# An MoE kernel in a hand-ordered schedule: counts that go from the scan to the triangular product, weights asked for at step 2, other pauses between engines, small products in banks of their own

## The chip, the cores and the metric

One core of one Trainium2 chip runs the whole program once. The metric is device microseconds of one launch. A profile is one further launch with the hardware profiler on; its times are taken from that launch alone.

## What is computed

Three layers follow one another on 14336 tokens of 192 numbers each (4 sequences of 3584).

```python
# 1  causal convolution over 7 tokens, one softmaxed filter per head (8 heads of 24)
out = einsum('hk,bskhg->bshg', softmax(weight), x_unf)
# 2  first MoE, on the tokens with x @ w_skip > 0 only; the others pass as they are
e_idx = argmax(xc @ w_gate); gate_w = softmax prob of e_idx
y[mask e] = gate_w * (relu(xc @ w1[e]) @ w2[e]); out = xc + y
# 3  second MoE, on all tokens
logits = x @ w_gate + modality_bias[modality_id]
out[mask e] = gate_w * (relu(x @ w1[e]) @ w2[e])
```

Each MoE has 8 experts with w1 of 192 x 1024 and w2 of 1024 x 192, and picks one expert for a token. All inputs are float32.

## The kernel before

**Data.** Products run in float16 with a high and a low part of each operand. The experts' weights are therefore prepared on the chip: for each expert the sum of squares is found by products of the weights with themselves (`gram`, a PSUM region), a power of two is taken from it as a scale, and the weights are split into a high and a low part (`w1b`, `w2b` for layer one, three buffers of each; `o` for layer two), which are also stored to DRAM (`s1a`, `s2a`, `s1b`, `s2b`) for the jobs that load them later.

**Stages.** The first phase (`Phase1.run`) goes through 64 convolution steps v (8 groups of 16 token tiles, 8 heads each) and 12 more to empty its pipeline: step v transposes the tiles of v - 9 (`tr`), convolves head v % 8 of group v // 8 (`conv`), and makes the gate products of v - 11 (`gm`); `lows` is VectorE's part, `fin` the gate decision of one group. Then `Ffn.run` goes through jobs of 128 tokens of one expert: 56 jobs of layer one and 6 overflow jobs (n1 = 62), then the jobs of layer two, first the tokens that skipped layer one (B), then those that came out of it (A). The first 12 jobs (experts 0 to 3, three jobs each) use tokens of the first four groups only, so that they can start before the first phase is through; jobs 12 to 55 take experts 1 to 7 and then 0. Each job is two first products with their evictions (`mm1`), and the second product of the job before (`mm2`).

**Order.** VectorE, ScalarE, TensorE and GpSimd execute their instructions in the order in which the program emits them (`InOrder`); SyncE, which issues the DMAs, is ordered by the compiler's scheduler. Background work is written as Python generators: a `yield n` lets n ticks pass. The first phase gives two ticks per step; `bg`, which a job calls four times, runs one step of the first phase while there are any left (`"x" not in w`), with that step's two ticks, and then ticks the queues `tk` (gates, routing) and `tkw` (weights) itself: `tk` twice in the first 12 jobs until the full routing is known, else once, `tkw` once. So the pauses fix where, among the products, each small operation stands in its engine's queue; an operation that is not ready there holds up all that is behind it on that engine.

**Routing.** `route_a` takes the gate codes of one group, compares them with the 8 experts (`oh`), scans the result over experts and tiles (`cum`, one running sum through all of them), and needs for each expert how many tokens of it lie in lower partitions: a product of the per-partition counts with a strictly triangular matrix (`tri`), and with ones for the totals. The counts are differences of neighbouring ends of the running sum, made on GpSimd (`genda`, `cnta`). From the product come ranks, slots and the index lists `la` (after 4 groups) and `ls` (after 8). `ranks` is the same for the other routes, on VectorE.

**Weights.** `prep` is one lane of weight preparation. For each expert in its list: loads (`loadt`, `loadr`, `load2`, the next expert's while the present one is split), products for the sums of squares, `dg` and `ssq` on VectorE, a product with ones, `pow2`, then the split in eight steps with `pace` ticks between, then the two stores. Lane 0 starts in step 8 of the first phase, lane 1 when the first phase is over (`late_pools`). A split waits for a free buffer (`guard`) and for the other lane's split (`busy`). If job i needs an expert of layer one that is not split yet, `pre` ticks `tkw` until it is: all that was still to come is then emitted at once, ahead of the job's products. At the end of job 56 (`i == n1 - 6`) `tk.drain` and `tkw.drain` do the same with whatever is left, and the pools of the second lane are given back.

**Banks.** PSUM has 8 banks, here `bk[0]` to `bk[7]`. Two engines' accesses to one bank are ordered one after the other, whichever columns they touch.

## Time and profile before

| | |
|---|---|
| three runs | 1071.69, 1083.71, 1078.73 us; median 1078.73 |
| the profiled execution | 1078.92 us, span 1077.1 us, mean granted clock 0.941 |
| busy: TensorE, VectorE, GpSimd, ScalarE | 967.9, 688.7, 628.5, 501.1 us |
| weight loads on TensorE (beside its products) | 802.2 us |
| DMA | 165.35 MB, mean 154 GB/s |

The span goes from the first to the last instruction; the execution's own time is 1.8 us longer. Busy time is the sum of the instructions of an engine. The granted clock is TensorE's: 1.00 is 2.4 GHz, and a stretch at 1.2 GHz counts 0.5. In the rows below PE is TensorE, DVE VectorE, ACT ScalarE, POOL GpSimd, SP SyncE; an operation is written as out<-in with the names of the program's tiles (`bank` is any PSUM bank), partitions x elements and type; what stands in brackets is the engine's idle time before it and who ended that. Nearly all instructions bear line 70, that of the helper that emits them, so tiles tell them apart.

### The profile page before, as it was taken

Reading aid. Unit: us, or ns where it says so; the run is one execution under the profiler, and the core shown is the slowest. Engines: PE = TensorE matmul, PEld = TensorE weight load, DVE = VectorE, ACT = ScalarE, POOL = GpSimd, SP = SyncE. Lnnn points to the kernel's source line nnn. Section 1 sums busy time; section 2 is a strip of 40 time slices with the busy share of each in tenths; the row PEclk is TensorE's granted clock in tenths of the full one; section 3 lists DMA queues with packets and bytes.
Section 4 is the critical chain, followed back from the end, with each engine's and each line's share of the span. In section 5 each row is a group of like instructions: output and inputs, shape, how many; then the busy total and the mean of one; then the engine's idle time right before and its main releaser. Section 6 shows DMA issues by size and latency. Waiting matters only on the chain. (4 is left out here: it accounts for less than half of the span.)

```text
span 1077.1 us, 27331 instructions
## 1 busy us (share of the span) xinstructions
PE 967.9 (90%) x10104; PEld 802.2 (74%) x10104; DVE 688.7 (64%) x1797; ACT 501.1 (47%) x919; POOL 628.5 (58%) x1113
## 2 busy tenths in 40 slices
PE   6688877799999879999899999999999899999993
PEld 4556666688888767888777877778787788888882
DVE  4376966769998889888446666667844344444441
ACT  3485743443665535455345555553233333333331
POOL 4044778776856836676447877774443555545531
PEclk9887876999999889999999999999999999999997
DMA  5666457665669737767973443333257333323340
GB/s 203 210 205 246 153 169 217 172 199 160 208 181 267 229 121 244 221 204 219 292 229 98 95 110 101 96 101 91 53 151 242 78 73 75 76 72 72 79 117 14
DMA packets 109135, 165.35 MB, mean 154 GB/s; under 512 B 80976, under 2 KB 86074, under 8 KB 103233
## 3 DMA queue, kind: packets, MB, share of 16 engines
q1 hardware_dynamic: 94368, 134.02, 39.9%
q0 software_dynamic: 13920, 28.87, 11.9%
q8 instruction: 81, 1.33, 0.5%
q10 hardware_dynamic: 704, 0.63, 0.2%
q14 instruction: 62, 0.50, 0.2%
HBM read 181.56 MB, written 58.42 MB: 223 GB/s over the span
## 5 line engine op out<-in xcount | busy, mean ns | idle before, releaser
L70 PEld LDWEIGHTS <-w1b 128*128 128x128 f16 x4840 | 374.4, 100 | 54.1 <-issue 18.5
L70 PE MATMUL bank<-xp,w1b 128*128 128x256 f16 x2200 | 263.7, 273 | 8.2 <-DMA w1b<-s1b 2.5
L70 PEld LDWEIGHTS <-ws 128*128 128x128 f16 (+2 forms) x2208 | 192.1, 100 | 67.0 <-DMA ws<-in_moe_w_dram 10.9
L70 PE MATMUL bank<-w2b,ws 128*128 128x384 f16 x1760 | 237.4, 286 | 0.2 <-issue 0.2
L70 DVE SCALAR_TENSOR_TENSOR ws<-bank,ws 128x512 f16<-128x512 f32 x220 | 151.4, 690 | 124.3 <-ACT ws L70 105.6
L70 POOL DMA_INDIRECT out_dram<-u,si x114 | 115.4, 1013 | 185.2 <-DVE u L70 58.7
L70 ACT ACTIVATE ws<-bank 128x512 f16<-128x512 f32 x220 | 130.6, 597 | 113.5 <-PE bank L70 102.7
L70 PE MATMUL bank<-xt,w1b 128*128 128x128 f16 x2640 | 170.1, 225 | 10.7 <-DVE hlo L70 6.9
L70 PE MATMUL bank<-w2b,hh 128*128 128x384 f16 x528 | 141.2, 334 | 1.0 <-DMA w2b<-s2a 1.0
L70 PE MATMUL bank<-w2b,hlo 128*128 128x192 f16 x528 | 131.8, 250 | 0.0
L70 ACT ACTIVATE u<-bank,c 128x192 f32<-128x192 f32 x114 | 48.1, 422 | 153.2 <-PE bank L70 118.1
L70 DVE SCALAR_TENSOR_TENSOR hlo<-bank,hh 128x512 f16<-128x512 f32 x132 | 90.3, 686 | 42.2 <-ACT hh L70 41.3
L70 DVE SCALAR_TENSOR_TENSOR u<-bank,c,u 128x192 f32<-128x192 f32 x114 | 47.6, 417 | 100.5 <-ACT u L70 84.5
L70 ACT ACTIVATE hh<-bank 128x512 f16<-128x512 f32 x132 | 76.7, 593 | 42.1 <-PE bank L70 40.7
L70 PEld LDWEIGHTS <-hh 128*128 128x128 f16 x528 | 53.4, 101 | 31.5 <-issue 3.3
L70 POOL DMA_INDIRECT gt<-rows,idx x64 | 64.0, 999 | 11.2 <-issue 9.3
L70 PE MATMUL bank<-xg,band 128*112 128x384 f32 x128 | 64.0, 593 | 0.3 <-DVE s L70 0.3
L70 ACT COPY xtb<-bank 128x672 f16<-128x672 f16 x64 | 46.5, 728 | 36.9 <-PE bank L70 36.5
L70 POOL DMA_INDIRECT gt<-rows,idxB x56 | 56.5, 1008 | 11.9 <-issue 7.0
L70 POOL TENSOR_TENSOR x2s<-x2s,xs 128x192 f32<-128x192 f32 x46 | 31.6, 688 | 53.7 <-DVE x2s L70 42.2
L70 PE MATMUL bank<-ob,oa 128*128 128x56 f16 (+2 forms) x446 | 49.7, 263 | 6.0 <-DVE ob L70 6.0
L70 PEld LDWEIGHTS <-hlo 128*128 128x128 f16 x528 | 52.9, 100 | 1.6 <-issue 1.5
(252 smaller groups left out, 1431.8 us busy)
## 6 DMA issues: line engine op xcount, KB each, us to landing
w1b<-s1b SPq DMA_DIRECT2D x59, 1024.0 KB
w2b<-s2b SPq DMA_DIRECT2D x59, 768.5 KB
ws<-in_moe_w_dram SPq DMA_DIRECT2D x16, 768.0 KB
rows<-hl SPq DMA_DIRECT2D x8, 1386.0 KB
xg<-in_x_dram SPq DMA_DIRECT2D x7, 1536.0 KB
ws<-in_moe_w_dram SPq DMA_DIRECT2D x16, 512.0 KB
ws<-in_moe_w_dram SPq DMA_DIRECT2D x32, 256.0 KB
s1a<-w1b SPq DMA_DIRECT2D x8, 1024.0 KB
```

What stands on the lines that cost most here:

```text
L70: r = f(*args, **kw)
```

## The change

In `route_a` and `ranks` the last column of the running sum itself goes into the two products, and the differences are taken of the results, after the copy out of PSUM (`off`, `po`, with a zero column in front). The first lane starts in step 2 and pauses 26 ticks before its first product, where it started in step 8 and paused 14; the second lane pauses 14 where it paused 8. Between VectorE's sums of squares and the product with ones lie 5 ticks (3 before), then 3 (2), then 3 (1) to the split. While layer one's jobs run and the first phase is not over, the split takes 2 ticks a step (1). `tk` is ticked twice a call only once the first phase is over. Expert 6 of layer two goes from the second lane's end to the first lane's end. `res["A"]`, which lets the next group's routing start, is set ahead of a pause. The second lane's sums of squares and the small routing products go to bank 4, and the last gate sums from bank 5 to bank 4. An unused region is dropped.

```diff
--- before.py
+++ after.py
@@ -33,7 +33,7 @@
 SB = 7
 NSA = E * SB
 XA = 16
-LANES = [(0, e) for e in range(E)] + [(1, 7)], [(1, e) for e in range(7)]
+LANES = [(0, e) for e in range(E)] + [(1, 7), (1, 6)], [(1, e) for e in range(6)]
 RW = 396
 MB = 192
 CAP = 120
@@ -124,16 +124,15 @@
         self.py = [bk[2][:, :2 * D]]
         self.py2 = bk[6][:, :2 * D]
         self.acc = [bk[3], bk[5]]
-        self.pt, self.pt2 = [h[4][:, 0:384]], [h[7][:, 512:896], h[3][:, 0:384]]
+        self.pt2 = [h[7][:, 512:896], h[3][:, 0:384]]
         self.pg2 = [bk[5][:, i:i + 64] for i in (0, 64, 128)]
-        self.gram = [bk[7][:, 256:512], bk[7][:, 0:256]]
-        self.misc = bk[3][:, 496:512]
+        self.gram = [bk[7][:, 256:512], bk[4][:, 0:256]]
+        self.misc = bk[4][:, 496:512]
         self.ph3 = bk[5]
         self.misca = bk[3][:, 240:256]
         self.pc0 = [bk[i][:TP, :384] for i in (5, 0, 1)]
         self.ptr0, self.ptr1 = ([h[i][:, :6 * TP] for i in p] for p in ((6, 2), (6, 5)))
-        self.pgt0, self.pgt1 = ([bk[i][:, 0:136] for i in p] for p in ((7, 4), (7,)))
-        self.pgt1.append(bk[5][:, 352:488])
+        self.pgt0, self.pgt1 = ([bk[i][:, 0:136] for i in p] for p in ((7, 4), (7, 4)))
         self.gramx = bk[3][:, 384:512]
         self.scm = bk[3][:, 256:384]
         self.cp = ctx.enter_context(tc.tile_pool(name="cp", bufs=1))
@@ -279,7 +278,7 @@
         nc.vector.tensor_scalar(out.bitcast(I32), q.bitcast(I32), -0.5, float(0x5F3759DF), ALU.mult, ALU.add)
         nc.vector.tensor_scalar(out.bitcast(I32), out.bitcast(I32), EXPM, None, ALU.bitwise_and)
 
-    def prep(self, ws, pool, pq, dst, guard, done, es, lane, lag, pace, free, busy):
+    def prep(self, ws, pool, pq, dst, guard, done, es, lane, lag, pace, free, busy, first):
         nc = self.nc
         g = self.gram[lane].rearrange("p (i c) -> p i c", i=2)
         sq = g[:, 0, 0:2]
@@ -301,7 +300,7 @@
             return w2t
 
         nxt = (loadt(*es[0]), loadr(*es[0])), load2(*es[0])
-        yield lag()
+        yield first
         for n, (q, e) in enumerate(es):
             (wt, wr), w2t = nxt
             for i, vs in enumerate(((wt,) * 8 + (wr[0:64],) * 8, (w2t,) * 12)):
@@ -315,13 +314,13 @@
             nc.vector.tensor_tensor(dg, g, self.identf.unsqueeze(1).to_broadcast([128, 2, 128]), ALU.mult)
             ssq = pq.tile([128, 2], F32, name="ssq")
             nc.vector.tensor_reduce(ssq, dg, AX.X, ALU.add)
+            yield 5
+            nc.tensor.matmul(sq, self.ones, ssq, start=True, stop=True)
             yield 3
-            nc.tensor.matmul(sq, self.ones, ssq, start=True, stop=True)
-            yield 2
             sc = pq.tile([128, 2], F32, name="wsc")
             self.pow2(sq, sc)
             nc.vector.tensor_scalar(sc, sc, 2.0 ** 30, 2.0 ** FT, ALU.min, ALU.mult)
-            yield 1
+            yield 3
             while not guard(q, e) or busy[0]:
                 yield 1
             busy[0] = True
@@ -361,15 +360,15 @@
             nc.vector.scalar_tensor_tensor(o1[:, 3, F // 2:], wr[:, F // 2:], sc[:, 0:1], o1[:, 2, F // 2:], ALU.mult, ALU.subtract)
             done[q].add(e)
             busy[0] = False
-            yield 2 + q
+            yield 2
             nc.sync.dma_start(ws[q][2][e], o1)
-            yield 2 + q
+            yield 2
             nc.sync.dma_start(ws[q][3][e], o2.bitcast(I32))
-            yield 2 + q
+            yield 2
             if q:
                 free[0] = None
             if not last:
-                yield max(1, lag() - 3 * (2 + q))
+                yield max(1, lag() - 6)
 
     def route_a(self, g, code, pool, ob, res):
         nc = self.nc
@@ -398,20 +397,21 @@
         gend = pool.tile([128, 9], F32, name="genda")
         nc.gpsimd.memset(gend[:, 0:1], 0.0)
         nc.gpsimd.tensor_copy(gend[:, 1:9], cum[:, :, GT - 1])
-        cnt = pool.tile([128, 8], F32, name="cnta")
-        nc.gpsimd.tensor_tensor(cnt, gend[:, 1:9], gend[:, 0:8], ALU.subtract)
+        off = pool.tile([128, 2, 9], F32, name="offa")
+        nc.gpsimd.memset(off[:, :, 0:1], 0.0)
         pos = pool.tile([128, GT], F32, name="posa")
         nc.gpsimd.tensor_scalar(pos, cg, -float(SB * 128), float(8 * SB * 128), ALU.mult, ALU.add)
+        yield 4
+        pp = self.misca
+        nc.tensor.matmul(pp[:, 0:8], self.tri, cum[:, :, GT - 1], start=True, stop=True)
+        nc.tensor.matmul(pp[:, 8:16], self.ones, cum[:, :, GT - 1], start=True, stop=True)
         yield 3
-        pp = self.misca
-        nc.tensor.matmul(pp[:, 0:8], self.tri, cnt, start=True, stop=True)
-        nc.tensor.matmul(pp[:, 8:16], self.ones, cnt, start=True, stop=True)
-        yield 2
-        off = pool.tile([128, 16], F32, name="offa")
-        nc.vector.tensor_copy(off, pp)
+        nc.vector.tensor_copy(off[:, :, 1:9], pp.rearrange("p (k c) -> p k c", k=2))
+        cnt = pool.tile([128, 2, 8], F32, name="cnta")
         nc.gpsimd.tensor_tensor(gend[:, 0:8], base, gend[:, 0:8], ALU.subtract)
-        nc.gpsimd.tensor_tensor(gend[:, 0:8], gend[:, 0:8], off[:, 0:8], ALU.add)
-        nc.gpsimd.tensor_tensor(base, base, off[:, 8:16], ALU.add)
+        nc.gpsimd.tensor_tensor(cnt, off[:, :, 1:9], off[:, :, 0:8], ALU.subtract)
+        nc.gpsimd.tensor_tensor(gend[:, 0:8], gend[:, 0:8], cnt[:, 0], ALU.add)
+        nc.gpsimd.tensor_tensor(base, base, cnt[:, 1], ALU.add)
         if g == GA - 1:
             nc.gpsimd.tensor_scalar(base[:, 0:EA], base[:, 0:EA], float(SA * 128), None, ALU.max)
         nc.gpsimd.tensor_tensor(cum, cum, gend[:, 0:8].unsqueeze(2).to_broadcast([128, 8, GT]), ALU.add)
@@ -437,8 +437,8 @@
         nc.gpsimd.tensor_tensor(q, pos, tf, ALU.add)
         nc.gpsimd.tensor_tensor(ok[:, 0], ok[:, 0], cg, ALU.mult)
         nc.gpsimd.tensor_tensor(cg, cg, ok[:, 0], ALU.subtract)
+        res["A"] = g + 1
         yield 5
-        res["A"] = g + 1
         for h in (2 * g, 2 * g + 1):
             u = slice(8 * (h % 2), 8 * (h % 2) + 8)
             a = ob.tile([128, 128, 8], F16, name="oa", bufs=2)
@@ -478,7 +478,7 @@
         nc.vector.tensor_scalar(idx, ei, 127.0, None, ALU.add)
         res.update(idx=idx, va=va)
 
-    def ranks(self, code, pool, lag, r, wait=4):
+    def ranks(self, code, pool, lag, r, wait=6):
         nc = self.nc
         T = code.shape[-1]
         oh = pool.tile([128, 8, T], F32, name="rA")
@@ -490,17 +490,18 @@
         gend = pool.tile([128, 9], F32, name="gend")
         nc.vector.memset(gend[:, 0:1], 0.0)
         nc.vector.tensor_copy(gend[:, 1:9], cum[:, :, T - 1])
-        cnt = pool.tile([128, 8], F32, name="cnt")
-        nc.vector.tensor_tensor(cnt, gend[:, 1:9], gend[:, 0:8], ALU.subtract)
+        po = pool.tile([128, 2, 9], F32, name="po")
+        nc.vector.memset(po[:, :, 0:1], 0.0)
         yield wait
         pp = self.misc
-        nc.tensor.matmul(pp[:, 0:8], self.tri, cnt, start=True, stop=True)
-        nc.tensor.matmul(pp[:, 8:16], self.ones, cnt, start=True, stop=True)
+        nc.tensor.matmul(pp[:, 0:8], self.tri, cum[:, :, T - 1], start=True, stop=True)
+        nc.tensor.matmul(pp[:, 8:16], self.ones, cum[:, :, T - 1], start=True, stop=True)
         yield 2
-        off = pool.tile([128, 17], F32, name="off")
-        nc.vector.tensor_copy(off[:, 0:16], pp[:, 0:16])
-        nc.vector.tensor_tensor(off[:, 0:8], off[:, 0:8], gend[:, 0:8], ALU.subtract)
-        r.extend((oh, cum, off[:, 0:8], off[:, 8:16]))
+        nc.vector.tensor_copy(po[:, :, 1:9], pp.rearrange("p (k c) -> p k c", k=2))
+        off = pool.tile([128, 2, 8], F32, name="off")
+        nc.vector.tensor_tensor(off, po[:, :, 1:9], po[:, :, 0:8], ALU.subtract)
+        nc.vector.tensor_tensor(off[:, 0], off[:, 0], gend[:, 0:8], ALU.subtract)
+        r.extend((oh, cum, off[:, 0], off[:, 1]))
         yield 1
 
     def qsl(self, pos, pool, tag=""):
@@ -922,7 +923,7 @@
         nc.vector.tensor_scalar(s.bitcast(I32), mx.bitcast(I32), EXPM, EXPM, ALU.bitwise_and, ALU.bitwise_xor)
         nc.vector.tensor_scalar(ef.bitcast(I32), mx.bitcast(I32), EXPM, None, ALU.bitwise_and)
         nc.vector.scalar_tensor_tensor(mt[:, :, 0], ef, 0.5, mt[:, :, 0], ALU.mult, ALU.mult)
-        yield 1
+        yield 3
         for k in range(nb):
             nc.scalar.activation(x2[:, k, :], x2[:, k, :], AF.Copy, scale=s[:, k:k + 1])
             yield 1
@@ -1150,7 +1151,7 @@
                     return True
                 return False
 
-            return m.prep(ws, w["pw2"] if k else pw, pq, dst, guard, (d1, d2), LANES[k], k, lambda: 8 if k else 8 if late() else 14, lambda: 1 if late() else 3, owner, conv)
+            return m.prep(ws, w["pw2"] if k else pw, pq, dst, guard, (d1, d2), LANES[k], k, lambda: 8 if k else 8 if late() else 14, lambda: 3 if not late() else 1 if "x" in w else 2, owner, conv, 14 if k else 26)
 
         def routes():
             while "idx" not in ls:
@@ -1180,7 +1181,7 @@
             if v == 1:
                 nc.sync.dma_start(rows[0:128, :], m.dz.bitcast(I32))
                 nc.sync.dma_start(rows2[0:128, :], m.dz.bitcast(I32))
-            if v == 8:
+            if v == 2:
                 tkw.add(lane(0))
             if routed[0] < p1.codes:
                 tk.add(m.route_a(routed[0], m.code[:, 0, :], rt, ob, ra))
@@ -1299,7 +1300,7 @@
                     tk.add(m.route(m.codeA[:, 0:NC], NS2A, "2", rt, ob, l2, np=NP2A))
                     tk.drain()
             if i < n2:
-                for _ in range(2 if i < EA * SA and "idx" not in ls else 1):
+                for _ in range(2 if i < EA * SA and "idx" not in ls and "x" in w else 1):
                     tk.tick()
                 tkw.tick()
                 tk2.tick()
```

## Rows read from the trace of the kernel before

**Rows 1.** The page, TensorE's busy tenths in 40 equal slices.

```profile
PE   6688877799999879999899999999999899999993
```

**Rows 2.** TensorE's waits, 24 to 60 us: total us, times, longest.

```profile
PE bank L70 <- DMA ws<-in_moe_w_dram: 8.2, 2, 7.1
```

**Rows 3.** TensorE in order of time: start, us, operation, count, idle before.

```profile
43.87 1.46 PE L70 MATMUL bank<-ws 128*128 128x128 bf16 x12 [7.09 <-DMA ws<-in_moe_w_dram]
...
53.39 0.86 PE L70 MATMUL bank<-xg,band 128*112 128x384 f32 x2
...
74.96 1.58 PE L70 MATMUL bank<-xg,band 128*112 128x384 f32 x2
```

**Rows 4.** Six windows: busy PE, PEld, DVE, ACT, POOL (instructions), clock, DMA share, GB/s.

```profile
34.00:45.00 11.00, 2.85 (x40) 2.42 (x39) 1.10 (x5) 1.42 (x3) 0.00 (x0) 0.75 1.00 326
45.00:59.80 14.80, 14.33 (x152) 9.85 (x150) 7.86 (x25) 10.38 (x17) 2.84 (x4) 0.84 0.19 62
59.80:143.90 84.10, 70.94 (x721) 52.28 (x721) 66.77 (x200) 55.56 (x92) 50.22 (x144) 0.82 0.64 221
110.00:126.20 16.20, 13.86 (x160) 10.62 (x160) 15.28 (x44) 14.38 (x24) 13.09 (x33) 0.96 0.39 121
158.30:187.20 28.90, 22.05 (x224) 20.36 (x225) 17.24 (x46) 10.67 (x15) 24.07 (x64) 0.58 0.84 236
500.00:525.00 25.00, 25.00 (x330) 21.88 (x328) 17.13 (x45) 11.23 (x25) 15.97 (x33) 1.00 1.01 300
```

**Rows 5.** TensorE's waits, 0 to 225 us.

```profile
PE bank L70 <- POOL cnta L70: 14.3, 6, 3.1
PE bank L70 <- DMA ws<-in_moe_w_dram: 9.9, 4, 7.1
...
PE bank L70 <- DVE L L70: 3.2, 2, 2.7
```

**Rows 6.** TensorE's waits, 345 to 425 us.

```profile
PE bank L70 <- DVE ssq L70: 6.8, 1, 6.8
```

**Rows 7.** TensorE's waits, 520 to 560 us.

```profile
PE bank L70 <- DMA xt<-gt: 3.0, 1, 3.0
PE bank L70 <- DMA w1b<-s1b: 2.5, 1, 2.5
```

**Rows 8.** SyncE's queue in order of time: when a DMA was issued.

```profile
25.81 0.33 SPq L1181 DMA_DIRECT2D rows<-rC  x1
...
28.51 0.52 SPq L667 DMA_DIRECT2D xg<-in_x_dram  x1
...
29.59 0.69 SPq L300 DMA_DIRECT2D ws<-in_moe_w_dram  x1
```

**Rows 9.** VectorE in order of time, 56 to 112 us.

```profile
68.06 0.41 DVE L70 TENSOR_TENSOR_SCAN cuma<-oha 128x128 f32<-128x128 f32 x1
```

**Rows 10.** GpSimd in order of time, 56 to 112 us.

```profile
70.67 0.74 POOL L70 TENSOR_TENSOR cnta<-genda 128x8 f32<-128x8 f32 x1
```

**Rows 11.** TensorE in order of time, 143 to 230 us.

```profile
179.32 1.91 PE L70 MATMUL bank<-ws 128*128 128x128 bf16 x16
```

**Rows 12.** ScalarE, 488 to 516 us: three passes of one expert's split.

```profile
488.43 1.03 ACT L70 CAST o<-ws 128x1024 f16<-128x1024 f32 x1
...
492.93 0.94 ACT L70 ACTIVATE o<-ws,wsc 128x768 f16<-128x768 f32 x1
...
494.55 1.15 ACT L70 ACTIVATE o<-ws,wsc 128x1024 f16<-128x1024 f32 x1
```

**Rows 13.** VectorE, 488 to 516 us.

```profile
498.62 0.74 DVE L70 SCALAR_TENSOR_TENSOR o<-ws,wsc,o 128x512 f16<-128x512 f32 x1
...
509.91 0.54 DVE L70 TENSOR_REDUCE ei<-rC 128x56 f32<-128x224 f32 x1
...
513.34 0.18 DVE L70 TENSOR_SCALAR idxB<-ei 128x56 int32<-128x56 f32 x1
```

**Rows 14.** TensorE, 505 to 525 us: the first product of one job.

```profile
511.24 2.40 PE L70 MATMUL bank<-xt,w1b 128*128 128x128 f16 x40
```

## The prediction

> **What bounds the kernel now.** I read the page first, then the stages by windows, then TensorE's waits in each stage, then the order in time around the longest of them. On the page TensorE's slices fall below 9 mainly in the first sixteen of forty, and from the middle on it is all but full [rows 1]: time is to be had early, not late. What is late there differs by stage. Up to step 16 of the first phase it is the first expert's weights: TensorE stands 8.2 us for them [rows 2], 7.1 us of it in one piece that ends at 43.87 us [rows 3]. From step 25 to 62 (59.8 to 143.9 us) it works 70.9 of 84.1 us at a mean clock of 0.82 [rows 4]; its largest wait is for the small count tile that GpSimd makes for the routing [rows 5]. In the first jobs (158.3 to 187.2 us) it works 22.1 of 28.9 us at 0.58 [rows 4]. After that single waits remain: VectorE's sums of squares at 400 us [rows 6], DMA at jobs 60 to 62 [rows 7]. The clock is the second loss: the same convolution pair takes 0.86 us at the upper level (2.4 GHz) and 1.58 us at the lower one (1.2 GHz) [rows 3], and the low stretches follow the stalls. A stall removed early therefore pays twice, and a stall added costs twice.
>
> **First weights (gain 9 us).** TensorE asks for them at the same step as before: 26 half-steps after step 2 is where 14 after step 8 was. Only their place in SyncE's queue moves. There the zero rows, which wait for GpSimd, are issued at 25.81 us; then come the weights, with the load of token group 3 among them at 28.51 us, and the second matrix only at 29.59 us [rows 8]. The change puts all four weight transfers ahead of group 3, but not ahead of the zero rows, so they start at some 27 us as now. What they gain is that 1.5 MB of group 3 no longer share the DMA engines with them: at the 326 GB/s that these move when full [rows 4] that is 4.8 us, and the rest of what overlaps can only add to it. I take 6.5 us of the 8.2, and 2.5 us for the clock: 0.84 over the 14.8 us that follow the wait [rows 4] is 0.16 x 2 x 14.8 = 4.7 us at the lower level, of which half is lost. Ends 0 and 11.
> The Trainium skill (DMA: Bandwidth & Descriptors, section Queues, rings and completion order) says that a DMA engine consumes the descriptors of a ring in ring order. By that alone nothing issued later could hold the second matrix up, all 8.2 us would go, and the sum below would be 1061. No run here shows that order by itself.
>
> **Counts straight from the scan (gain 13 us).** Today the triangular product waits for GpSimd's copy and difference: the scan on VectorE starts at 68.06 us and takes 0.41 [rows 9], the difference on GpSimd starts at 70.67 and takes 0.74 [rows 10], because GpSimd is still busy with the next group's gate inputs. This costs TensorE 14.3 us in six waits [rows 5]. Afterwards the product needs only the scan and stands one tick later, so these waits go. What is late next is VectorE: it works 66.8 of the 84.1 us of this stage, and in the group from 110.0 to 126.2 us, at clock 0.96, it worked 15.28 of 16.2, or 94% [rows 4]. At 94% the 66.8 us need 71, so the stage can lose 13 us; 17 if it had no gap at all. At the lower end two thirds of the 14.3 us go (five of the eight groups make their product in this stage, and others wait too), 9.5 us, and VectorE takes 2.5 back, since one GpSimd subtraction, 0.74 us where it stood before, now stands between the product and the rank: 7 us. I take 13, by the group that ran least disturbed.
>
> **Banks and spacing in the first jobs (gain 12 us).** The last gate sums leave bank 5, into which the transposes also write, and the 3.2 us of waits for L go; so does the rest of the counts' 14.3 [rows 5]. Fewer ticks a call (three, not four) thin out what ScalarE and VectorE get per job. The 28.9 us hold 22.1 us of work, some of it at the lower level [rows 4]; a clock that stayed up would halve the stretch. The latency from the routing to job 0's gather is shortened by nothing here. I take 6; ends 0 and 14. Lane 1's first products wait for loads that were asked for late, 9.9 - 8.2 = 1.7 us [rows 2, 5]; its longer first pause covers them: 2 with what the clock loses. The ones product of 400 us waits 6.8 us for sums of squares [rows 6], and two ticks more, of four a job, cover a part; but the prepared weights now meet the routing of layer two at other places. I take 4; ends -4 and 11. Gains: 9 + 13 + 12 = 34.
>
> **What the pacing takes (cost 11 us).** By the pauses of lane 0: before, expert 3's products run in job 1 [rows 11], its split ends in job 6, and job 9 is the first to use it. Afterwards expert 2 is split at two ticks a step over eight steps, most of them after the first phase has ended, where a call gives one tick; it ends in job 4. Six ticks of stores, two of pause and 15 from the products to the split put expert 3's split at the end of job 9, so that job 9 forces the last pauses and all eight steps into the queues ahead of its own first product. ScalarE then runs, behind the epilogue of job 7, six passes in a row, three of 1024 columns (1.15, 1.03, 1.15 us) and three of 768 (0.94 at most) [rows 12]: 6.1 us, 5.6 with their overlap. Ahead of them stand the epilogue and the power of two on VectorE, an estimated 1.5 us from operations of 0.2 to 0.4 us, and behind them VectorE's first half of the low part, 0.74 us [rows 13]. TensorE has one small product in that time: 8 us idle. The clock adds 3, as after the 7.1 us above. Ends 5 (if ScalarE has run ahead) and 14.
>
> **Expert 6 of layer two (cost 7 us).** It moves from lane 1 to the end of lane 0. By the same count its products come in job 56, and the rest is forced there, where the pools change. Its ones product stands behind VectorE's end of the route, which lies between 509.91 and 513.34 us today [rows 13], and its own sums: about 4 us of idle TensorE. Then 5.6 us on ScalarE and 1.5 us on VectorE stand ahead of job 57's evictions, covered by one job's two products, 2.40 us for the first [rows 14] and about 2 for the second: 3 to 4 us more. Its two stores (1.79 MB) fall into a stretch whose DMA share is already 1.01 [rows 4]. Against it, TensorE stands there today for 3.0 and 2.5 us [rows 7], which a later TensorE partly absorbs. I take 7; ends 0 and 14. Expert 7's split ends one call ahead of job 45: nothing, or 2 us if VectorE is behind. The longer pause before the scaling uses 8 of 16 ticks where it used 6, and costs nothing. Layer two's jobs, full now, stay as they are.
>
> **Sum.** 34 - 18 = 16 us off the profiled execution's own 1078.92 us (the span of 1077.1 and 1.8 around it): 1063 us. The median of the three runs, 1078.73, is the same number; they spread over 12 us, and about 1% is what a measurement of this kernel can tell from no change.
>
> **Rivals.** No change: VectorE and ScalarE already bound the first phase, and the removed waits come back as waits for evictions. The counts then give 7 us, the weights 6, the first jobs 4, and the costs stay at 18: 1079 - 17 + 18 = 1080. The 94% of one group speak for it, the 79% of the whole stage against. Weights not moved: SyncE's queue is not in the order of the program (group 3, asked for first, stands behind weights in it [rows 8]), so the first half of the change may do nothing: 9 us are missing, 1072. Slower: the prepared weights fall behind as a whole; the burst at job 9 draws lane 1's first expert into the same queues, and the one at job 56 puts its stores ahead of the reloads for jobs 59 to 64. At the upper ends, 14 and 14, with 5 for two late reloads, against gains of 7 + 2 - 4 = 5, it is 1079 + 33 - 5 = 1107; it decides from about 11 us more cost than gain on, and its middle is 1092. Clock: it stays at the upper level from step 16 to job 9, and the stages give 11, 17, 14, 2 and 4: 1079 - 48 + 18 = 1049.
>
> **How the numbers follow.** Forecast (1054 to 1070) 0.45; no change 0.19; weights not moved 0.12; slower 0.11; clock 0.13. The time is the forecast's 1063. The range leaves out half of the slower case, a third of the clock case and the outermost of the rest: 1045 to 1087. Faster by over 1%, under 1068: nine tenths of the forecast, nearly all of the clock case and a little of the third, 0.55. Slower, over 1089.5: 0.11. Between: 0.34.
>
> **What would show it.** Right: no wait of TensorE for counts; under 2 us for the first second matrix; step 62 by about 122 us; a gap of some 8 us ahead of job 9 with ScalarE full of weights and a low clock behind it; the same, smaller, at job 57. Wrong: groups that still take 16 us and more, with VectorE waiting for GpSimd's cumulated counts; no gap at job 9, because the forced work finds its engines ahead; larger gaps at jobs 58 to 64 than now.

## The result

The changed kernel takes 1087.67 us in the median of nine runs (1085.50 to 1093.80), the kernel before 1077.56 on the same chip (nine runs, 1071.69 to 1083.71): a ratio of 1.0106, 95% interval 1.0074 to 1.0139. It is 1% slower, where 1063 us were forecast. Its profiled execution took 1088.47 us, with a span of 1086.6 us and a mean granted clock of 0.954 (0.941 before), so the clock is not where the time went.

TensorE's busy tenths on the page of the changed kernel, and its granted clock below them:

```profile
PE   6889768879899788998799999999998999999992
...
PEclk9999869989999998999899999999999999999996
```

Slices 2 and 4 are fuller than in [rows 1]; of slices 9 to 20, which hold the jobs of layer one from about job 9 on, seven are below 9 where three were. TensorE's waits from 0 to 225 us of the changed kernel (us in total, times, longest):

```profile
PE bank L70 <- DMA xt<-gt: 8.3, 1, 8.3
PE bank L70 <- DVE offa L70: 8.1, 4, 3.6
...
PE bank L70 <- DMA ws<-in_moe_w_dram: 4.6, 4, 1.5
...
PE bank L70 <- ACT w1b L70: 4.1, 2, 3.2
...
PE bank L70 <- DVE L L70: 1.3, 1, 1.3
```

Against [rows 5] the wait for the count tile is gone, the weights cost 4.6 us for 9.9, and L 1.3 for 3.2. New are the wait for job 0's gathered tokens (8.3 us in one piece) and that for the copy `offa` out of PSUM: 8.1 us, where the count tile had cost 14.3. In order of time, what the first-weight part and job 0 became:

```profile
38.83 1.46 PE L70 MATMUL bank<-ws 128*128 128x128 bf16 x12 [1.54 <-DMA ws<-in_moe_w_dram]
...
149.28 0.93 PE L70 MATMUL bank<-xt,w1b 128*128 128x128 f16 x7 [8.25 <-DMA xt<-gt]
```

The first of these answers to the 7.09 us of [rows 3]. Windows of the changed kernel (columns as in [rows 4]); the first answers, to about 1 us, to its stage from 59.8 us on, the second is the way from step 62 to job 0, and the last two are the stretches behind job 10 and from job 56 on:

```profile
51.80:125.60 73.80, 63.92 (x737) 47.19 (x735) 61.10 (x191) 56.59 (x94) 48.64 (x137) 0.95 0.58 199
125.60:149.30 23.70, 10.22 (x141) 8.81 (x141) 11.49 (x37) 7.20 (x12) 18.45 (x51) 0.74 0.85 276
...
228.50:501.80 273.30, 247.93 (x3155) 216.47 (x3152) 236.62 (x552) 140.10 (x251) 178.99 (x257) 0.96 0.70 196
501.80:543.10 41.30, 30.00 (x357) 26.15 (x354) 22.76 (x53) 17.97 (x33) 19.66 (x32) 0.88 0.86 269
```

The starts of the same products in both time orders cut the span into stages. Each entry is a difference of two starts, in us; "before, again" is a second trace of the kernel before (experiment 11).

| stage | before | before, again | changed | changed less before |
|---|---|---|---|---|
| start to step 62 | 144.2 | 138.6 | 125.6 | -18.6 |
| step 62 to job 0 | 14.2 | 15.2 | 23.7 | +9.5 |
| job 0 to job 8 | 71.2 | 67.4 | 53.9 | -17.3 |
| job 8 to job 10 | 12.8 | 12.7 | 25.3 | +12.5 |
| job 10 to job 56 | 264.7 | 267.2 | 273.3 | +8.6 |
| job 56 to the first pair of layer two's jobs | 33.2 | 33.3 | 41.3 | +8.1 |
| first pair to pair 54 | 497.3 | 491.5 | 502.2 | +4.9 |
| rest | 39.5 | 39.5 | 41.2 | +1.7 |

Against the second trace of before the lead at step 62 is 13.0 us, and layer two's jobs lose 10.7; pairs 34 to 54 take 165.7 us in every trace, so what these jobs lose lies ahead of them.

At job 8 the changed kernel leads by 26.3 us, near the 30 of the forecast's terms up to there (9, 13, 6 and 2). The five stages behind it give back 35.8. Two of them hold the bursts, the stretches in which forced weight work stands ahead of the products. The first burst is also the other side of the gain ahead of it, since the split that it forces was not done in jobs 0 to 8: jobs 0 to 10 together take 79.2 us, where the two traces of before have 84.0 and 80.1. At job 9 (TensorE in order of time):

```profile
215.65 0.58 PE L70 MATMUL bank<-ssq,ones 128*128 128x2 f32 x2 [2.22 <-DVE ssq L70]
217.13 0.40 PE L70 MATMUL bank<-xt,w1b 128*128 128x128 f16 x2 [0.90 <-ACT w1b L70]
220.70 0.39 PE L70 MATMUL bank<-xt,w1b 128*128 128x128 f16 x2 [3.18 <-ACT w1b L70]
223.21 2.96 PE L70 MATMUL bank<-xt,w1b 128*128 128x128 f16 x27 [2.12 <-DVE w1b L70]
```

and at job 57, where VectorE's four halves of expert 6 stand ahead of its evictions (TensorE, then VectorE):

```profile
520.77 4.43 PE L70 MATMUL bank<-xt,w1b 128*128 128x128 f16 x40 [8.55 <-DVE hlo L70]
```

```profile
516.62 3.51 DVE L70 SCALAR_TENSOR_TENSOR o<-ws,wsc,o 128x384 f16<-128x384 f32 x4 [4.45 <-ACT o L70]
520.04 1.28 DVE L70 SCALAR_TENSOR_TENSOR hlo<-bank,hh 128x512 f16<-128x512 f32 x2
```

From job 10 to job 56 no wait stands out. TensorE's waits there, in the changed kernel (228.5 to 501.8 us), and then in the kernel before (242.3 to 507.0 us):

```profile
PE bank L70 <- DVE hlo L70: 10.8, 10, 2.5
PE bank L70 <- DVE ob L70: 6.2, 7, 2.5
PE bank L70 <- DVE po L70: 2.5, 1, 2.5
PE bank L70 <- DVE ssq L70: 2.0, 1, 2.0
```

```profile
PE bank L70 <- DVE ssq L70: 7.4, 2, 6.8
PE bank L70 <- DVE hlo L70: 6.9, 5, 2.4
PE bank L70 <- DVE ob L70: 2.7, 4, 1.4
```

The sums of squares are waited for less, as forecast; evictions (`hlo`) and the routes' lists (`ob`) more, in many small pieces, and always for VectorE.

### The profile page after: what moved, and what is told of

It reads as the page before. It is cut to its first block, busy times and chain, and to the rows that moved or that the text cites. A ratio compares the mean times of both kernels' runs of the same rounds, so it can differ in the third digit from the quotient of the medians.

```text
span 1086.6 us, 27334 instructions
## 1 busy us (share of the span) xinstructions
PE 957.6 (88%) x10104; PEld 794.5 (73%) x10104; DVE 693.5 (64%) x1800; ACT 501.0 (46%) x919; POOL 629.0 (58%) x1121
## 4 chain that ended last, share of the span: by engine, by line
PE 45%; DVE 15%; ACT 5%; DMA 4%; issue 4%; SPq 1%; POOL 1%; POOLq 0%; ACTq 0%; DVEq 0%
PE bank L70 45%; DVE hlo L70 2%; DMA out_dram<-u,si 2%; DVE o L70 2%; ACT ws L70 2%; DVE ws L70 1%; DVE rC L70 1%; DVE mx L70 1%; DVE ob L70 1%; ACT o L70 1%; ACT hh L70 1%; DMA gt<-rows,idxB 1%; DMA w1b<-s1b 1%; DVE c L70 1%; SPq L842 1%
## 5 line engine op out<-in xcount | busy, mean ns | idle before, releaser
L70 PEld LDWEIGHTS <-ws 128*128 128x128 f16 (+2 forms) x2208 | 188.4, 99 | 62.5 <-DMA ws<-in_moe_w_dram 5.4
L70 PE MATMUL bank<-xt,w1b 128*128 128x128 f16 x2640 | 172.6, 226 | 36.6 <-DVE hlo L70 20.2
L70 ACT ACTIVATE x2s<-bank,c 128x192 f32<-128x192 f32 x46 | 19.4, 421 | 110.6 <-DVE c L70 59.9
L70 PEld LDWEIGHTS <-oa 128*128 128x128 f16 x446 | 44.6, 152 | 20.7 <-issue 17.4
L70 PE MATMUL bank<-xg,band 128*112 128x384 f32 x128 | 57.9, 541 | 2.0 <-DVE hl L70 1.6
```

What stands on the lines that cost most here:

```text
L70: r = f(*args, **kw)
```

## The experiments

Each kernel was timed against the kernel before on the chip it ran on. The chips differ (that median was 1077.9 us for experiments 1 to 4, 1071.6 for 5 to 8, 1070.9 for 9 to 12, 1070.1 for 13 to 16, 1079.8 for 17, 1072.4 for 18), so ratios are compared, not times. For the stretch from job 9 to job 56 the two traces of the kernel before, from two chips, give 271.5 and 273.9 us, so that stage can be compared between traces to some 3 us.

**1. The pauses put back.**

```diff
# changed kernel
-            yield 5
+            yield 3
             nc.tensor.matmul(sq, self.ones, ssq, ...)   # then 2 for 3, 1 for 3
-            yield 2          # behind each store
+            yield 2 + q
```

> The changed kernel, with the pauses inside the weight preparation as they were (3, 2 and 1 ticks around the product with ones, 2 + q after the split). Counted in ticks, expert 3's split then ends by itself in job 6 and expert 6's of layer two in job 55, so neither is forced. Theory (the two forced bursts cost more than the early gain): job 9 starts some 25 us ahead of the kernel before instead of 18, and keeps it; no loss at jobs 57 to 59; 1060 to 1070 us. Rival (the later loss comes from elsewhere, such as the double tick withheld, the banks or the second route): 1080 to 1088, with the loss between jobs 9 and 12 still there. Rival (the longer pauses were needed, because the product with ones waits for VectorE's sums of squares): the bursts go, but waits of 5 to 10 us for those sums come in their place; 1075 to 1085.

1085.30 us, ratio 1.0070 (1.0035 to 1.0104). Both bursts are gone, as the theory said: from job 8 to job 10 it takes 14.8 us, and no split stands ahead of job 57 (yet from job 56 to the first pair it takes 38.5 us, before 33.2). The time is hardly better. Jobs 9 to 56 still take 284.5 us, with 14.6 us of waits for sums of squares and 13.8 for evictions (7.4 and 6.9 before). The theory that the bursts are the whole cause falls.

**2. Expert 6 back in the second lane.**

```diff
-LANES = [(0, e) for e in range(E)] + [(1, 7), (1, 6)], [(1, e) for e in range(6)]
+LANES = [(0, e) for e in range(E)] + [(1, 7)], [(1, e) for e in range(7)]
```

> The changed kernel, with expert 6 of layer two back at the end of the second lane. Step of the prediction (moving expert 6 to the first lane is what forces its split at job 56): the loss of 13 us around jobs 57 to 59 goes, and 1076 to 1081 us are left. Theory after counting ticks (the longer pauses alone delay either lane by so much that the split is still not done at job 56): the loss stays where it is, 1084 to 1090.

1088.70 us, 1.0127 (1.0084 to 1.0171): the time of the changed kernel. The longer pauses, not the lane, put expert 6 behind job 56; in its old lane the four halves are forced as well, but TensorE waits 3.37 us for the eviction behind them instead of 8.55.

**3 and 4. The early half alone, the longer pauses alone,** both in the kernel before. 

```diff
# 3: route_a and banks as changed, and
-            if v == 8:
+            if v == 2:              # first pauses 26 and 14
# 4
-            yield 3
+            yield 5                 # then 3 for 2, 3 for 1, and 2 behind each store
```

> The kernel before, with the early half of the change alone: counts of the first routing straight from the scan (with the earlier release of the next group), weights asked for at step 2, the banks. Pauses, pace, ticks, lanes and the other routes as before. Theory: step 62 some 18 us earlier as in the changed kernel, job 9 some 20 to 26 us earlier, nothing given back behind it; 1053 to 1062 us. Rival (the lead is lost in the latency between the first phase and the jobs, and in waits for evictions): job 9 at most 12 us earlier, 1066 to 1072. Rival (a stalled stretch further on takes it back whatever the start): 1075 or more.

1085.29 us, 1.0071 (1.0033 to 1.0110).

> The kernel before, with only the longer pauses inside the weight preparation (5, 3 and 3 ticks around the product with ones, 2 after the split in both lanes). Theory (they make the two bursts): expert 3's last four ticks are forced ahead of job 9, less than in the changed kernel, for 3 to 8 us; expert 6's split is forced at job 56, for 8 to 13 us; with 3 to 5 us saved at the sums of squares near 400 us, 1084 to 1094 us. Rival (pauses relieve waits and the forced work is covered): 1068 to 1078.

1100.41 us, 1.0224 (1.0191 to 1.0257). Each half makes the kernel slower by itself, and both stretch jobs 9 to 56, to 282.4 and 284.8 us. With the pauses alone that is mostly the burst at job 9: jobs 8 to 10 take 20.2 us, 7.5 more than before, and jobs 10 to 56 268.8, little more than before (264.7 and 267.2). In the early half 18.7 us of lead at step 62 are 11.0 at job 9 and 0.1 at job 56, though of the pauses of the weights and the later routes one alone was touched: the second lane's first, 14 for 8.

**5 to 8. The parts of the early half,** in the kernel before: banks; counts of `route_a`; weights at step 2 with the second lane left at 8; the last two together.

```diff
# 5
-        self.misc = bk[3][:, 496:512]
+        self.misc = bk[4][:, 496:512]      # and gram, pgt1
# 6 and 8
-        nc.tensor.matmul(pp[:, 0:8], self.tri, cnt, ...)
+        nc.tensor.matmul(pp[:, 0:8], self.tri, cum[:, :, GT - 1], ...)
# 7 and 8
-            if v == 8:
+            if v == 2:              # first pauses 26 and 8
```

> The kernel before with the moves of banks alone. Theory (order of ticks decides, and it is unchanged here): the 3.2 us of waits for L in the first jobs shrink, 1073 to 1079 us. Rival (bank 4 is now shared by lane 1's sums, the gate sums and the small routing products, and they wait for one another): the jobs 9 to 56 take 5 us or more longer than 271.5, 1081 to 1088.

0.9997 (0.9957 to 1.0036); jobs 9 to 56 take 271.2 us. The banks do nothing that can be told from no change.

> The kernel before with the first routing's counts straight from the scan alone (and the next group released ahead of the pause). The ticks of everything behind the first phase stay within one of those of before. Theory (the early lead is real and is lost only where the order of VectorE's work in the jobs is disturbed): step 62 is 9 to 13 us earlier, job 9 some 8 us, and jobs 9 to 56 take 271 to 275 us as before; 1066 to 1072. Rival (VectorE bounds the jobs, so that whatever the first phase gains is waited away by job 45): the lead at job 56 is under 2 us; 1075 to 1083.

1.0015 (0.9980 to 1.0050), no gain where the theory wanted some 0.5 to 1%. Step 62 is at 130.0 us, 8.6 ahead of the second trace of before; job 0 follows 21.4 us later instead of 15.2. Jobs 9 to 56: 273.9 us.

> The kernel before with the first lane begun at step 2 with its 26 ticks alone; the second lane pauses 8 as before, so that every tick from step 15 on is the same as before. Theory (order decides): a lead of 5 us at step 16 that is kept whole, 1070 to 1074 us. Rival (a lead is waited away): 1076 to 1080, with the lead gone by job 45.

0.9962 (0.9930 to 0.9994); jobs 9 to 56: 273.3 us.

> The kernel before with both early gains, weights at step 2 for the first lane alone and counts of the first routing from the scan; banks, second lane, pauses, pace and other routes as before. Theory (order decides, and the order behind the first phase is unchanged but for one tick): 18 us of lead at step 62, some 12 at job 9, kept to job 56; 1063 to 1069 us. Rival (a lead is waited away): as the run of the whole early half, 1080 to 1086, with jobs 9 to 56 taking 280 us or more. Between the two, 1070 to 1079, the banks or the second lane's first pause would account for the rest of that run's loss.

0.9970 (0.9938 to 1.0003), also less than the theory wanted; jobs 9 to 56: 274.7 us. With the order kept, what lead there is at job 9 is kept within 4 us to job 56 in all four: VectorE does not wait it away. But the counts' 8.6 us are gone by job 9 (at 228.2 us in 6, at 227.2 in the second trace of before).

**9 and 10. One number.** 9 is the kernel before with the second lane's first pause at 14; 10 is experiment 3 with that pause at 8.

```diff
-        yield lag()          # second lane: 8
+        yield first          # second lane: 14
```

> The kernel before with one number changed: the second lane's first pause, 14 ticks for 8. Counted in ticks, the second lane's splits end in jobs 11, 18, 25, 32, 39, 46 and 55 where they ended in 9, 16, 23, 30, 37, 44 and 53, and the first lane waits 1.5 jobs for its turn behind them. Theory (the order of the splits among the jobs is what turned the early half's 11 us of lead at job 9 into nothing at job 56): jobs 9 to 56 take 277 to 284 us for 271.5, and the time is 0.6 to 1.1% above the kernel before. Rival (the banks made that loss): within 0.3% of the kernel before.

1085.57 us, 1.0123 (1.0073 to 1.0172).

> The whole early half (weights at step 2, counts of the first routing, banks) with the second lane's first pause left at 8, so that it differs from the run of the early half by this number alone. Theory (order of the splits): the lead at job 9, some 12 us, is still 9 to 12 us at job 56; 0 to 0.8% under the kernel before. Rival (the banks): as the early half, 0.4 to 1.1% above it.

1066.14 us, 0.9944 (0.9918 to 0.9971). Six ticks of one generator, one and a half jobs, are worth 1.2 to 1.3%, in the kernel before and in the early half alike. Jobs 9 to 56 take 278.1 us in 9 and 273.9 in 10. So of the 13 us that experiment 9 loses, 4 to 7 lie in these jobs; another 4 lie between job 56 and the first pair (37.2 us for 33.2).

**11. The kernel before, traced again.**

> The kernel before itself, for a second trace. If stage lengths can be compared between traces, jobs 9 to 56 take 268 to 275 us again and step 62 stands within 4 us of 144.2. If they take 279 us or more, a stage length says little, and only times can be compared. The ratio is 1.000 within its interval in any case.

1.0014 (0.9977 to 1.0052). Jobs 9 to 56 repeat (273.9); the first phase differs by 5.6 us, more than expected, with nearly the same waits at another granted clock. Leads in the first phase are therefore known to some 6 us only.

**12. All counts from the scan,** added to experiment 8, with the wait of `ranks` at 4.

```diff
-        nc.tensor.matmul(pp[:, 0:8], self.tri, cnt, ...)
+        nc.tensor.matmul(pp[:, 0:8], self.tri, cum[:, :, T - 1], ...)
```

> The run of weights and counts with the second lane at 8, and the counts of the later routes taken straight from the scan too, with their wait left at 4 ticks. Theory: the product for the second of these routes waits for one VectorE operation less; the 4.0 us wait for the count tile near 362 us gets shorter by 1 us or not at all, because VectorE is behind there as a whole; the same 0.3% under the kernel before, within 0.3. Rival (the difference operation was the delay): that wait goes, another 2 to 4 us, 0.5 to 0.8% under it.

1063.87 us, 0.9932 (0.9897 to 0.9967); jobs 9 to 56: 270.7 us. The wait near 362 us, 4.0 us in experiment 8, is 2.6 and now for the running sum itself. The ratio is the rival's, but the wait gives 1.4 us only, and the interval overlaps that of experiment 8.

**13 and 14. Splits back in their jobs; the first split alone late.** Both take the six ticks out behind the second lane's first expert; 13 is the changed kernel with pauses and lanes of before and that lane's first pause at 8, 14 the kernel before with it at 14.

```diff
-            yield 2 + q
+            yield 1 if lane and n == 0 else 2 + q     # three times
```

> The changed kernel with the pauses and lanes of before, the second lane's first pause at 8, and six ticks taken out behind its first expert, so that from its second expert on every split stands in the job where the kernel before has it (16, 19, 23, 26 and so on); pace, withheld double tick, counts, banks and the early weights stay as changed. Theory (the place of the splits is the whole cause): job 9 starts 15 us or more ahead, jobs 9 to 56 take 271 to 277 us, jobs 56 to 62 no more than 34; 0.6 to 1.6% under the kernel before. Rival (the other routes, which now begin two jobs later, or the longer pause before the scaling, do it as well): jobs 9 to 56 take 280 us or more, 0.4% under to 0.8% above it.

1069.81 us, 0.9995 (0.9969 to 1.0020). The slowdown is gone, the gain does not come: jobs 9 to 56 take 278.2 us, between the two expectations. 9.0 us of lead go in job 12, where the late first split meets the route (3.5 us for `po`, 2.2 for an eviction).

> The kernel before with the second lane's first pause at 14, and the six ticks taken out again behind its first expert: only the first split is late (job 11 for 9). If the first split's meeting with the second routing is what the run with the pause of 14 paid for, it loses 4 to 7 us between jobs 9 and 14 and keeps that: 0.4 to 0.8% above the kernel before. If the later splits' places (and the end of the last one at job 55) are, it is within 0.3% of it.

1.0058 (1.0031 to 1.0086). The first split's meeting with the route costs about half of experiment 9: 6.7 us between jobs 12 and 13, kept to the end.

**15 and 16. The joined version; the second lane early.** 15 is experiment 12 with the banks; 16 the kernel before with the second lane's first pause at 4.

```diff
# 16
-        yield lag()          # second lane: 8
+        yield first          # second lane: 4
```

> Weights at step 2, all counts straight from the scan, and the banks, with every tick of the weights as before. The runs of its parts were 0.6 and 0.7% under the kernel before. Theory (these gains lie in the first phase and the routes, and the banks add nothing of their own): 0.5 to 1.0% under it. Rival (the banks take waits away that the others left): 1.0 to 1.5% under it.

1062.64 us, 0.9932 (0.9904 to 0.9959); jobs 9 to 56: 271.2 us.

> The kernel before with the second lane's first pause at 4 for 8: its splits end one job earlier (8, 15, 22, 29, 36, 43, 52), the first lane's later ones half a job. If lateness is what costs, it is 0 to 0.5% under the kernel before. If the places among the jobs were fitted to each other, any shift costs, and it is 0.4 to 1.2% above it, with waits for evictions in jobs 9 to 56.

1.0082 (1.0046 to 1.0117); jobs 9 to 56: 276.2 us. Early costs too, but mostly in another way: 5.7 us of some 9 are a wait ahead of those jobs, the second lane's products standing for their loads in job 4. Jobs 9 to 56 lose only 2.3 to 4.7 us, so it is not shown that early is as dear there as late.

**17 and 18. The two other pauses,** added to experiment 15.

```diff
-    def ranks(self, code, pool, lag, r, wait=4):
+    def ranks(self, code, pool, lag, r, wait=6):     # 17 alone
-        yield 1
+        yield 3          # before the scaling; 17 and 18
```

> The joined version (early weights, all counts, banks, order of the splits as before) with the two longer pauses of the change added: 6 ticks in the counts of the later routes and 3 before the scaling. Pace and double tick as before. Theory (pace and withheld tick take the 0.7%, since they move the start of the second lane and of the routes among the jobs): these pauses cost nothing, 0.5 to 1.0% under the kernel before. Rival (the pauses take it): 0.3% under to 0.2% above it.

1081.78 us, 1.0042 (1.0003 to 1.0080).

> The joined version with the longer pause before the scaling alone (3 ticks for 1, with the routes' counts at 4). Step of the prediction (this pause costs nothing): 0.5 to 1.0% under the kernel before, as the joined version. Rival (the scaling comes 14 times between jobs 17 and 61, every fourth job, and two ticks later it meets the splits): jobs 17 to 45 lose 5 us or more against the joined version, 0.2% under to 0.5% above the kernel before.

1061.26 us, 0.9880 (0.9834 to 0.9926): the fastest ratio of the study, on six runs. The pause before the scaling costs nothing; two ticks in `ranks` take 1.6% between 17 and 18, and with that pause 1.1% between 17 and 15. Part of it is in a fixed place. From pair 25 to pair 26 of layer two's jobs, where route "2" makes its index lists (`ob`, `oa`), every kernel with `wait=6` takes 13.0 to 13.4 us (the changed kernel, 1, 2, 13, 17), and each of those with 4 takes 9.0. Part of that comes back beside it: from pair 20 to pair 27 the kernels with 6 take 81.5 to 83.8 us, those with 4 78.9 to 80.6. TensorE there, in experiment 17, and the window around it:

```profile
781.29 0.82 PE L70 MATMUL bank<-ob,oa 128*128 128x58 f16 x6 [1.69 <-DVE ob L70]
```

```profile
780.00:800.00 20.00, 18.71 (x159) 15.26 (x160) 9.59 (x24) 5.86 (x11) 7.04 (x9) 0.91 0.40 108
```

A wait of 1.69 us and a clock of 0.91 over 20 us (0.09 x 2 x 20 = 3.6 us at the lower level, half of them lost) make 3.5 of the 4 us. The larger part of 17's loss lies in jobs 17 to 43: 172.2 us, against 162.0 in 15 and 161.1 in 18.

## Why the prediction was wrong

**What bounds the kernel, and the first phase.** Right in direction. Step 62 was forecast 22 us earlier, by about 122 us, and came 18.6 earlier than in the trace the forecast was read from, at 125.6; 13.0 earlier than in the second. The weights moved as forecast and gave somewhat less: the second matrix's load is issued at 28.80 us and token group 3's behind it, at 29.49; TensorE's longest wait for weights is 1.54 us, its waits for them from 24 to 60 us fall from 8.2 to 3.6 us, where 6.5 were to go, and step 25 comes 7.1 us earlier (6.0 against the second trace) for the 9. When they were moved alone, 0.38% was left in the time, 4 us.

**The counts.** The 13 us were near at step 62 and wrong as a gain: from step 25 to step 62 the changed kernel takes 71.6 us, the two traces of before 83.0 and 78.5, and alone the counts are worth nothing in the time. VectorE, taken as 94% busy there, was busy 61.10 of 73.80 us, 83%. The prediction said that nothing shortens the latency from the routing to job 0's gather, but did not charge it. In the changed kernel that way grew by 9.5 us; in every kernel with counts from the scan it takes 21 us or more, in those without 14.1 to 15.2 (19.8 in experiment 4). Two pieces make the 9.5. The gather is issued 11.3 to 13.2 us after step 62 in the kernels with counts from the scan (13.2 in the changed one) and 8.7 to 9.8 in those without; why is open. The rest is the load that transposes the gathered tokens (`xt`), which now meets the first phase's store of its rows in SyncE's queue (the changed kernel, then the kernel before):

```profile
141.77 0.33 SPq L781 DMA_DIRECT2D rows<-hl  x1
142.21 8.63 SPq L842 DMA_TRANSPOSE xt<-gt  x3
```

```profile
155.88 1.31 SPq L841 DMA_TRANSPOSE xt<-gt  x1
157.28 0.51 SPq L780 DMA_DIRECT2D rows<-hl  x1
```

In all 13 traces where the store stands some 0.4 us ahead (the kernels with counts from the scan, and experiment 4), job 0 starts 6.4 to 7.7 us behind the transposing load; in the 7 where it stands behind, 2.5 us. No run moves that store by itself.

**The first jobs.** Mis-sized the other way: 17.3 us up to job 8 where 6 + 2 were taken. With the pauses put back it is 8.5 (62.7 us in experiment 1), so about half of it is split work put off to the burst.

**The bursts.** Both came in the places and through the engines forecast: 12.5 us between jobs 8 and 10 for 11, 8.1 from job 56 on for 7. The reason given for the second was wrong. It is the pauses that put expert 6 behind job 56; in its old lane it is forced too (experiment 2).

**The step that failed** is what the prediction took from the second lane and the routes between the bursts. It booked the second lane's longer first pause as a gain ("2 with what the clock loses") and the longer pauses before the ones product as 4 us of gain with an end of -4, and priced the two ticks in `ranks` not at all. Measured: that first pause alone costs the kernel before 1.2% (about 13 us, experiment 9), and the two ticks 1.1 to 1.6%. The longer pauses did shorten the waits for sums of squares (2.0 us for 7.4); alone they cost 2.2%, but about half of those 24 us is the two bursts, 7.5 and 5.6 us. From job 10 to 56 the changed kernel lost 8.6 us (6.1 against the second trace) instead of winning 4, and 4.0 at pair 25, of which part comes back beside it. Stage by stage against the forecast, that is 3.4 (to step 62), 9.5 (to job 0), -9.3 (to job 8), 1.5 (burst), 12.6 (jobs 10 to 56), 1.1 (job 56 on), 4.9 (layer two's jobs) and 1.7 (rest): 25.4 us, from 1063 to the 1088.5 of the profiled execution. The largest term is that of jobs 10 to 56. The prediction also had layer two's jobs stay as they are; they lost 4.9.

The runs fall into two groups by one number. Where splits and routes keep their places among the jobs (before twice, 5 to 8, 10, 12, 15, 18), jobs 9 to 56 take 270.7 to 274.7 us; where any of them is moved (changed, 1 to 4, 9, 13, 14, 16, 17), 276.2 to 287.8. The groups lie 1.5 us apart, less than two traces of one kernel differ, but only experiment 16 is so near; the next is 277.7. In the changed kernel, 2 and 4 the number holds the burst at job 9 too. The rival "no change" had the removed waits come back and the counts give 7 us: 8.1 us of waits for `offa` did come in place of 14.3, and the counts gave 11.4 or 6.9 us up to step 62, by the trace compared; its reason, waits for evictions, is not what is seen (1.3 us of them up to 225 us). That a lead is waited away later, as experiments 6 to 8 ask, is not seen either: leads survive when the order does. The rival of weights that stay where they were is out by the queue and the 1.54 us above, that of a clock that stays up by the 0.74 granted from step 62 to job 0. The slower rival had the sign and some of the size (1092) but another mechanism: behind job 57 the longest wait for a transfer is 2.8 us (3.0 in [rows 7]), and with both bursts taken out (experiment 1) the kernel is still 0.7% slower.

What a moved split meets can be read in experiment 9 at job 12. TensorE stands for an eviction; VectorE, ahead of it, has one half of a split (0.94 us) and two small operations, one of the route (`ns`) and one of the weights' scale (`wsc`), that take about three times as long as they do in the kernel before; GpSimd runs another pass of that split (TensorE, VectorE, GpSimd of experiment 9):

```profile
254.25 2.00 PE L70 MATMUL bank<-xt,w1b 128*128 128x128 f16 x18 [4.38 <-DVE hlo L70]
```

```profile
246.03 2.32 DVE L70 TENSOR_SCALAR ns<-off 128x8 int32<-128x8 f32 x1
...
249.40 1.09 DVE L70 TENSOR_SCALAR wsc<-wsc 128x2 int32<-128x2 int32 x2
...
252.66 0.94 DVE L70 SCALAR_TENSOR_TENSOR o<-ws,wsc,o 128x384 f16<-128x384 f32 x1
253.52 0.68 DVE L70 SCALAR_TENSOR_TENSOR hlo<-bank,hh 128x512 f16<-128x512 f32 x1
```

```profile
246.68 1.63 POOL L70 TENSOR_TENSOR o<-ws,o 128x768 f16<-128x768 f32 x1
```

The same operations in the kernel before, where the split was over before the route's counts came out:

```profile
246.91 0.66 DVE L70 TENSOR_SCALAR ns<-off 128x8 int32<-128x8 f32 x1
...
248.54 0.37 DVE L70 TENSOR_SCALAR wsc<-wsc 128x2 int32<-128x2 int32 x2
```

What stays open: which meeting costs what in the middle jobs, since only the first split's was isolated, and the meeting above was read from one trace; what pace and the withheld double tick are worth, which were never run by themselves; and why the pauses cost 2.2% in the kernel before but only about 0.4% in the changed one (between 1.0106 and experiment 1), where jobs 10 to 56 are even shorter with them (273.3 us for 279.6).

## What to carry to other kernels

In a schedule written in ticks, a pause is not a local cost: it moves everything its generator emits later against every other generator, and the price is paid where they meet, not at the pause. Before a pause is changed, list where each later piece of the queue lands among the jobs, and change it so that those places stay; here the same early gains were 0.7% slower with six ticks too many in one lane and 0.6% faster without them. A lead is worth only what reaches the next stage: follow it across the latency (a gather, a load) at the stage's end before booking it.

## What the runs showed of the hardware

A VectorE operation on 8 numbers per partition took 2.32 us in experiment 9, in the kernel before 0.66. GpSimd was in a pass of 768 columns meanwhile, and the operation ended at 248.35 us, as that pass did (246.68 + 1.63 = 248.31). Its row begins 0.65 us ahead of that pass, beside an earlier one. VectorE seems to stand until GpSimd's operation is through. The Trainium skill (SBUF — State Buffer, section Who interferes with whom) says that the two engines share a pair of ports, and that when VectorE works in a mode that uses both of its ports, whichever engine issues first has the pair for its whole instruction while the other fully blocks. The common end of the two rows agrees with it; which of them issued first, and in which mode VectorE worked, they do not show. If it holds, the place of a split's GpSimd passes matters to small VectorE operations that have nothing to do with it.

The first phase of the same kernel took 144.2 and 138.6 us in two traces with nearly the same waits (for the count tile 10.5 and 10.8 us up to 145 us); from 59.8 to 98.3 us the granted clock was 0.77 in the one, in the like stretch of the other (59.0 to 92.5 us) 0.95.
